# One core, cosformer attention followed by a swish MLP: chunk 1's output half plain and half in seven products, and another order and other stores for the last chunk

## The chip, the core and the metric

The kernel runs on one core of a Trainium2 chip. Its time is the device time of one launch in microseconds (us); lower is better. Engines are named as in the profile: PE (TensorE matmul), PEld (its weight load), DVE (VectorE), ACT (ScalarE), POOL (GpSimd) and SP (SyncE, which here only issues DMAs).

## What is computed

From q, k and v (8 batches, 8 heads, 576 positions, 64 features) a linear attention, whose result, 4608 tokens of 512, goes through an MLP with a swish whose slope is given by feature:

```python
r = np.maximum(x, 0.0); phi = np.concatenate([r * cos_w, r * sin_w], axis=-1)   # of q and of k
kv = np.einsum('bhsf,bhsd->bhfd', k_p, v); z = np.sum(k_p, axis=2)
attn = np.einsum('bhsf,bhfd->bhsd', q_p, kv) / (np.einsum('bhsf,bhf->bhs', q_p, z)[..., None] + 1e-06)
x = attn.transpose(0, 2, 1, 3).reshape(4608, 512)
h = x @ w_in                       # 512 -> 2048
g = h * (1.0 / (1.0 + np.exp(-beta * h)))
out = g @ w_out                    # 2048 -> 512
```

## The kernel before

**Chunks and batches.** The MLP works on 9 chunks (0 to 8) of 512 tokens; the attention on 8 batches of 576 tokens, which is nine blocks of 64. A batch is prepared while an earlier chunk is in the MLP. For a batch: q and k go through relu (L196, L199), v is scaled by cosine and sine (L202, 18 small pieces), relu(q) is transposed by a DMA on SP into `qt` (`q_turn_dma`, L251), `qs` is `qt` times a tangent (`tan_mul`, L221; by POOL in `q_tan`, L255, and for batch 2 by DVE at L827), `kv` is 144 small matmuls (`kv_mm`, L266), the attention's numerators are 144 more (`num_all`, L328, line L293 in the profile), and `x_part` (L779) divides them on DVE and sends them, transposed by a DMA on SP, into the chunk's `xt`.

**The MLP's two products.** A chunk makes 16 groups of `h` (128 features each), each followed by a silu on ACT into `g`, and then the output of four tiles of 128 tokens. A product is either plain (`h_group`, `h_plain`, `o_part`: matmuls of 512 columns) or by seven half-size products in place of eight (`h_fast`, `o_fast`: matmuls of 256 columns). For the latter DVE makes sums of the operands: S1 to S4 of `g` (`g_sum`, L390), T1 to T4 of `w_out` (`w_sums`, L803; T3 is written over a part of `wout`), and sums of `w_in` (`wh_sums`, L440) and of `xt`. `o_fast` (L536) returns named steps for one pair of token tiles (pair 0 is tiles 0 and 2, pair 1 tiles 1 and 3): "1" to "7" are products of eight matmuls on PE, c1, c5, cu and c4 are copies from PSUM by ACT, a2, a3 and a7 are additions on DVE that complete a part of the output and may release its store. "6", "7" and "4" add to the PSUM bank that "1" began, so "6" waits for c1, "7" for cu and "4" for a7.

**Which chunk does what.** Chunk 0 is plain. Chunk 1 makes `h` plainly (L811 to L827) and its output by two pairs of seven products (L840 to L865). Chunk 2 makes `h` plainly and its output by seven (L1014 to L1055). From chunk 3 on `chunk` (L917) walks a list written out by hand, `ORDER` for chunks 3 to 6 and `ORDER_END` for 7 and 8: a word such as `X6` is a step of an `h` pair, `p4` a plain group, `s12` a sum, `ox3` or `oy3` product "3" of output pair x (0) or y (1), `o3y` its a3 and `c4y` its c4. Each engine runs its instructions in the order of the program. Eight PSUM banks are shared by hand; the three numbers of a pair are the banks of "1/6/7/4", of "5/3" and of "2".

**Stores.** `store` (L506) writes a tile as two DMAs of 64 rows: from POOL up to chunk 6, then from SP; for the odd tiles of chunk 8 the second half is issued by ACT. In the last pair (`last`) c4 copies its 256 columns half by ACT and half by DVE, and a7's half of the tile is stored by itself.

**SPLITS** (L529) names, for chunks 2 to 5, how many groups of `h` and how many output products have their matmuls cut into two of half the columns: the same work in more instructions.

Of the kernel before, what the change touches and what calls it, by code (L numbers as in the profile page):

```python
# [13 lines left out]
ALU = mybir.AluOpType  # L14
PSUM = bass.MemoryType.PSUM

P = 128
NQ = 9
# [4 lines left out]
def kernel(  # L23
# [224 lines left out]
    def qs_of(b):  # L248
        return wx["q"] if b > 3 and b % 2 == 0 else qs_first
# [137 lines left out]
            gs[c, jt // 4] = gt_pool.tile([P, 4, TCH], BF16, name="g_t", tag="g_t")  # L387
        nc.scalar.activation(gs[c, jt // 4][:, jt % 4], ps[:, h_bank(c, jt)], AF.Silu, scale=beta[:, jt : jt + 1])  # L388

    def g_sum(c, i0, i1, kind):  # L390

        k_ = i0 // 2
        g_e, g_o = (gs[c, k_][:, 2 * (i0 - 2 * k_) + r : 2 * (i1 - 2 * k_) : 2] for r in range(2))
        hf = TCH // 2
        A11, A12, A21, A22 = g_e[:, :, 0:hf], g_o[:, :, 0:hf], g_e[:, :, hf:TCH], g_o[:, :, hf:TCH]
        s1, s2, s3, s4 = (t[:, i0:i1] for t in (S1, S2, S3, S4))
        o, l, r, op = {1: (s1, A21, A22, ALU.add), 2: (s2, s1, A11, ALU.subtract),
                       3: (s3, A11, A21, ALU.subtract), 4: (s4, A12, s2, ALU.subtract)}[kind]
        return nc.vector.tensor_tensor(o, l, r, op=op)  # L399

    def g_sums(c, i0, i1):
        for kind in (1, 3, 2, 4):
            got = g_sum(c, i0, i1, kind)
        return got

    def h_group(c, jt, cols=1):
# [33 lines left out]
    def wh_sums(jt):  # L440
        f0 = jt % 4
        A11, A12, A21, A22 = (win[jt // 4][:, 2 * jp : 2 * jp + 2, f * P : (f + 1) * P]
                              for f in (f0, f0 + 1) for jp in range(2))
        s1, s2, s3, s4 = (w_sum(jt, i) for i in range(4))
        nc.vector.tensor_tensor(s1, A21, A22, op=ALU.add)
        nc.vector.tensor_tensor(s3, A11, A21, op=ALU.subtract)
        nc.vector.tensor_tensor(s2, s1, A11, op=ALU.subtract)
        return nc.vector.tensor_tensor(s4, A12, s2, op=ALU.subtract)

    def x_sums(c):  # L450
        xt, n = xt_tile(c), NB // 2
# [51 lines left out]

    out_v = out.rearrange("(b p n) m -> b n p m", b=B, n=NQ)

    def store(c, tt, o_sb, m0=0, m1=DM):  # L506
        for hf in range(2):
            bb, n = divmod((c * TCH + tt * P) // HP + hf, NQ)
            eng = nc.gpsimd if c < 7 else (nc.sync, nc.scalar)[hf] if c == NTC - 1 and tt % 2 else nc.sync
            eng.dma_start(out=out_v[bb, n][:, m0:m1], in_=o_sb[hf * HP : (hf + 1) * HP, m0:m1])  # L510

    def o_mm(c, tt, jts, cols=1):
        o_ps = ps[:, (2, 3, 0, 1)[tt] if c == 0 else 2 + tt // 2]
# [12 lines left out]
    def o_part(c, tt, part, cols=1):  # L526
        o_mm(c, tt, range(4 * part, 4 * part + 4), cols)

    SPLITS = {2: (0, 11), 3: (5, 0), 4: (0, 8), 5: (3, 0)}  # L529
    made = {}  # L530

    def late(c):
# [3 lines left out]
    def o_fast(c, pr, banks):  # L536

        b_ps, e_ps, a_ps = (ps[:, k_, 0:HM] for k_ in banks)
        tok = slice(pr * P, (pr + 1) * P)
        last = c == NTC - 1 and pr == 1  # L540

        def prod(dst, left, right, start, stop, pieces=False):
            order = (0, 1, 2, 3, 4, 5, 7, 6) if c + 1 >= B else range(JT // 2)
            for i in order:
                w = HM // 2 if i and pieces else HM
                for m in range(0, HM, w):
                    nc.tensor.matmul(dst[:, m : m + w], lhsT=left(i), rhs=right[:, i, m : m + w],  # L547
                                     start=start and i == 0,
                                     stop=stop and i == order[-1], skip_group_check=True)

        def g_part(r, hf):
            def at(i):
                jt = 2 * i + r
                return gs[c, jt // 4][:, jt % 4, hf * (TCH // 2) + pr * P : hf * (TCH // 2) + (pr + 1) * P]
            return at

        def s_part(t):
            return lambda i: t[:, i, tok]

        o1 = osb_pool.tile([P, DM], FP32, name="o_sb", tag="o_sb")  # L560
        o2 = osb_pool.tile([P, DM], FP32, name="o_sb", tag="o_sb")
        p1 = part.tile([P, HM], FP32, name="p1", tag="p1")
        p5 = part.tile([P, HM], FP32, name="p5", tag="p5")
        u = part.tile([P, HM], FP32, name="u", tag="u")

        def c4():
            h = HM // 2 if last else HM
            nc.scalar.copy(o2[:, 0:h], b_ps[:, 0:h])
            if last:
                nc.vector.tensor_copy(o2[:, h:HM], b_ps[:, h:HM])  # L570
                store(c, pr + 2, o2, 0, HM)

        def stored(key, op):
            def do():
                op()
                waits[key[0]].discard(key[1:])
                if not waits[key[0]] and not (last and key[0] == "2"):
                    store(c, pr + (2 if key[0] == "2" else 0), o2 if key[0] == "2" else o1)
                if last and key == "2a7":
                    store(c, pr + 2, o2, HM, DM)  # L580
            return do

        waits = {"1": {"a2", "a3"}, "2": {"a7", "c4"}}
        add = dict(op=ALU.add)
        return {
            "1": lambda: prod(b_ps, g_part(0, 0), B11, True, False, late(c)),
            "5": lambda: prod(e_ps, s_part(S1), T1, True, False, late(c)),
            "6": lambda: prod(b_ps, s_part(S2), T2, False, False, late(c)),
            "2": lambda: prod(a_ps, g_part(1, 0), B21, True, True, late(c)),
            "7": lambda: prod(b_ps, s_part(S3), T3, False, False, late(c)),  # L590
            "3": lambda: prod(e_ps, s_part(S4), B22, False, True, late(c)),
            "4": lambda: prod(b_ps, g_part(1, 1), T4, False, True, late(c)),
            "c1": lambda: nc.scalar.copy(p1, b_ps),
            "c5": lambda: nc.scalar.copy(p5, e_ps),  # L594
            "cu": lambda: nc.scalar.copy(u, b_ps),
            "c4": stored("2c4", c4),
            "a2": stored("1a2", lambda: nc.vector.tensor_tensor(o1[:, 0:HM], a_ps, p1, **add)),
            "a3": stored("1a3", lambda: nc.vector.tensor_tensor(o1[:, HM:DM], e_ps, u, **add)),
            "a7": stored("2a7", lambda: nc.vector.tensor_tensor(o2[:, HM:DM], b_ps, p5, **add)),
        }  # L600
# [202 lines left out]
    def w_sums():  # L803
        z = ALU.subtract
        nc.vector.tensor_tensor(T1, B12, B11, op=z)
        nc.vector.tensor_tensor(T2, B22, T1, op=z)
        nc.vector.tensor_tensor(T4, B21, T2, op=z)
        nc.vector.tensor_tensor(T3, B22, B12, op=z)

    wx_tiles()  # L810
    for slot in range(16):  # L811
        h_group(1, slot)
        if slot == 0:
            num_rest()
            att_q(2)
            v_half(2, 0)
        if 3 <= slot < NQ:
            v_half(2, 1, slot, slot + 1, "act")
        if slot == 4:
            k_all(2)  # L820
            v_half(2, 1, 0, 3)
        elif slot == 6:
            w_sums()
        elif slot == 11:
            kv_all(2)
            for jp in range(2):
                tan_mul(nc.vector, qs_of(2)[:, jp], qts[0][:, jp], 0, NQ)  # L827
    q_relu(3, 0, "act")
    q_relu(3, 1, "act")
    q_turn_dma(3)  # L830

    def one_sums(kind):
        for i0 in range(0, JT // 2, 2):
            g_sum(1, i0, i0 + 2, kind)

    def ops(of, names):
        for n in names.split():
            of[n]()

    x, y = o_fast(1, 0, (2, 5, 4)), o_fast(1, 1, (3, 7, 6))  # L840
    ops(x, "1 c1")
    one_sums(1)
    ops(y, "1 c1")
    for t, bank in enumerate((4, 6, 0)):
        num_all(2, t, bank)
    one_sums(2)
    x_part(2, 0, 4)
    ops(x, "6 cu")
    ops(y, "6 cu")
    one_sums(3)  # L850
    ops(x, "2 5 c5")
    x_part(2, 1, 6)
    ops(x, "7")
    one_sums(4)
    ops(x, "a2 a7")
    ops(y, "7 2")
    got = wh_sums(0)
    x_part(2, 2, 0)
    load_raw(4, "q")
    q_tan(3, 0, got)  # L860
    q_tan(3, 1)
    ops(y, "a2 5 c5")
    ops(x, "3 a3 4 c4")
    ops(y, "a7 3 a3 4 c4")
    v_half(3, 0)  # L865

    def k_piece(b, j):
# [10 lines left out]
        "p7 s04 s13 V4 s22 SbV s23 sp7 s24 s31 s33 N0 k1 s32 ox1 c1o ox5 k3 c5o k2 ox6 s34 g0 g1 x0 k0 "  # L878
        "ox3 oy1 cuo c1y x2 o3x ox2 ox7 v8 oy5 x1 c5y o2x oy6 w8 q0 q1 cuy v2 v6 oy3 o7x v3 w1 oy7 w4 w3 "
        "w7 o7y ox4 v5 t3 w5 oy2 v4 c4x o3y v7 t1 w0 oy4 w6 t2 v1 c4y v0 o2y w2 t4")  # L880
    ORDER_END = (
        "E1 F1 E2 X1 c1E X5 c1X X2 E5 a2E c5X X6 E6 X3 c1F a2X Y1 cuX X7 c5E cuE c1Y E3 E7 Y6 a3X SaX cuY "
        "a7X a3E Y5 SaE a7E X4 F6 F5 Y7 c5Y E4 Y2 cuF c5F Y3 F7 F2 a7Y a3Y a7F SbX SbE Y4 F3 a2Y Z1 a2F "
# [33 lines left out]
    def chunk(c, b, x, y, parts):  # L917
# [22 lines left out]
            ({"q0", "q1"} | xs_all, q_next),  # L940
            ({f"{o}{n}" for o in "vw" for n in range(NQ)}, lambda: raw_next("v"))])
        last_sum = None
        for op in (ORDER if b < B else ORDER_END).split():
            n = int(op[-1]) if op[-1].isdigit() else None
            if op == "K":
                kv_mm(b, 0, 4)
# [59 lines left out]
    for c in range(2, NTC):  # L1006
        b = c + 1
        parts = (6, 0, 4) if c < FAST else (0, 6, 4)
        xb, yb = ((2, 3, 6), (1 if c == FAST - 1 else 7, 3, 6)) if c < FAST else ((3, 2, 0), (1, 2, 0)) if b < B else ((0, 3, 6), (1, 3, 6))
        x, y = o_fast(c, 0, xb), o_fast(c, 1, yb)  # L1010
        if c >= FAST:
            chunk(c, b, x, y, parts)
# [73 lines left out]
```

## Time and profile before

| | |
|---|---|
| median of 3 runs | 277.27 us (277.11 to 277.93) |
| the profiled execution | 277.93 us; span from first to last instruction 276.2 us |
| PE busy | 267.5 us (97%), 3745 matmuls |
| DVE, ACT, POOL busy | 221.2, 184.4, 67.8 us |
| granted TensorE clock | 1.000 |
| chunk 1: `h` groups, then output | 50.4 to 65.8 us, then 65.8 to 80.2 us |
| chunk 8: `h`, then output | 247.0 to 259.5 us, then 259.5 to 271.9 us |

The durations below come from the profiled execution, and times in us within it count from its first instruction. A busy PE is not yet PE at its peak, because the ends of matmuls are modelled; the distance from one matmul's start to the next is exact. The chain that ended last is followed back from the last instruction, at each step to what released it.

### The profile page before, as it was taken

What the parts mean: (1) busy time and instruction counts of PE and PEld (TensorE: products, weight loads), DVE (VectorE), ACT (ScalarE), POOL (GpSimd) and SP (SyncE); (2) the same over time, 40 slices, a digit from 0 to 9 for tenths busy, and PEclk for the clock granted to TensorE, in tenths of its full rate; (3) what the DMA queues carried; (4) which work ended last, traced back from release to release, by engine and by line L of the source; (5) the groups of instructions that cost most, each with busy time, mean ns of one, the idle gap of its engine ahead of it and who ended that gap; (6) DMA issues with size and microseconds to landing.
All of it is one profiled execution on the core that took longest, in us unless ns stands there. A gap on an engine that the chain in (4) does not pass through costs nothing.

```text
span 276.2 us, 9045 instructions
## 1 busy us (share of the span) xinstructions
PE 267.5 (97%) x3745; PEld 199.3 (72%) x3749; DVE 221.2 (80%) x579; ACT 184.4 (67%) x381; POOL 67.8 (25%) x87
## 2 busy tenths in 40 slices
PE   8799999999999999999999999999999999999993
PEld 8454455456875599869866898688768886888783
DVE  5989968599989899499958995899589589559832
ACT  5778757797238657697569856986595279439811
POOL 1444000600087073205520553044400140000000
PEclk9999999999999999999999999999999999999999
DMA  6999999999989999981899199905400740023006
GB/s 250 366 394 383 391 391 314 365 196 384 186 220 277 215 339 273 400 154 33 196 367 248 31 200 297 149 20 108 114 2 9 119 115 2 0 65 90 2 4 150
DMA packets 50585, 54.00 MB, mean 196 GB/s; under 512 B 31200, under 2 KB 31472, under 8 KB 50544
## 3 DMA queue, kind: packets, MB, share of 16 engines
q1 hardware_dynamic: 47584, 45.82, 60.2%
q0 software_dynamic: 2688, 7.34, 9.2%
q8 instruction: 29, 0.48, 0.8%
q10 hardware_dynamic: 272, 0.27, 0.4%
q14 instruction: 12, 0.10, 0.2%
HBM read 36.71 MB, written 9.44 MB: 167 GB/s over the span
## 4 chain that ended last, share of the span: by engine, by line
PE 80%; DMA 12%; DVE 3%; issue 1%; ACT 1%; SPq 1%; ACTq 0%; DVEq 0%
PE ps L547 31%; PE ps L468 16%; PE ps L422 13%; PE ps L380 11%; DMA raw_v<-in_v_dram 7%; DMA raw_q<-in_q_dram 5%; PE ps L293 3%; PE ps L517 3%; PE ps L272 2%; SPq L79 1%; DVE xs L315 1%; ACT vb L217 1%; PE ps L234 0%; PE ps L352 0%; DVE win L115 0%
## 5 line engine op out<-in xcount | busy, mean ns | idle before, releaser
L413 ACT ACTIVATE g_t<-ps,beta 128x512 bf16<-128x512 f32 x96 | 61.2, 699 | 2.9 <-DVE ps L498 2.8
L547 PEld LDWEIGHTS <-S 128*128 128x128 bf16 x589 | 51.3, 98 | 5.0
L510 POOL DMA_DIRECT2D out_dram<-o_sb x56 | 33.5, 604 | 66.6 <-ACT o_sb L523 24.6
L380 PE MATMUL ps<-xt,win 128*128 128x512 bf16 (+1 forms) x196 | 42.8, 375 | 0.1
L547 PEld LDWEIGHTS <-g_t 128*128 128x128 bf16 x440 | 38.2, 98 | 4.5 <-issue 0.4
L422 PE MATMUL ps<-xt,win 128*128 128x512 bf16 (+1 forms) x184 | 40.8, 351 | 0.0
L388 ACT ACTIVATE g_t<-ps,beta 128x512 bf16<-128x512 f32 x48 | 32.2, 690 | 7.9 <-PE ps L380 7.8
L380 PEld LDWEIGHTS <-win 128*128 128x128 bf16 x196 | 18.7, 98 | 21.1 <-issue 0.4
L547 PE MATMUL ps<-wout,g_t 128*128 128x256 bf16 (+1 forms) x284 | 31.8, 262 | 0.0
L547 PE MATMUL ps<-wout,S 128*128 128x256 bf16 (+1 forms) x305 | 31.5, 255 | 0.0
L547 PE MATMUL ps<-T,S 128*128 128x256 bf16 (+1 forms) x284 | 30.8, 262 | 0.0
L399 DVE TENSOR_TENSOR S<-g_t 128x512 bf16<-128x512 bf16 (+1 forms) x66 | 25.2, 412 | 4.1 <-ACT g_t L413 3.4
L217 ACT ACTIVATE vb<-raw_v,sin 128x256 bf16<-128x256 f32 (+1 forms) x61 | 27.4, 503 | 1.5 <-DMA raw_v<-in_v_dram 1.5
L222 POOL TENSOR_TENSOR qs<-qt,tanr 128x1152 bf16<-128x1152 bf16 x6 | 14.2, 2381 | 51.4 <-DVE den L304 29.8
L468 PEld LDWEIGHTS <-w_stage 128*128 128x128 bf16 x224 | 21.6, 98 | 6.9
L468 PE MATMUL ps<-w_stage 128*128 128x256 bf16 x168 | 26.5, 272 | 0.0
L422 PEld LDWEIGHTS <-win 128*128 128x128 bf16 x184 | 17.9, 98 | 10.1
L315 DVE TENSOR_TENSOR xs<-ps,rden 128x768 bf16<-128x768 f32 (+4 forms) x26 | 22.8, 884 | 0.8
L219 DVE TENSOR_SCALAR vb<-raw_v,cos 128x256 bf16<-128x256 f32 x63 | 20.6, 384 | 0.2
L594 ACT COPY p<-ps 128x256 f32<-128x256 f32 x16 | 6.0, 372 | 20.4 <-PE ps L547 20.4
L468 PEld LDWEIGHTS <-win 128*128 128x128 bf16 x168 | 16.4, 98 | 4.4 <-issue 0.4
L468 PE MATMUL ps<-xt,win 128*128 128x256 bf16 x112 | 19.1, 273 | 0.0
(106 smaller groups left out, 416.5 us busy)
## 6 DMA issues: line engine op xcount, KB each, us to landing
raw_v<-in_v_dram SPq DMA_DIRECT2D x7, 1152.0 KB, 10.3
raw_k<-in_k_dram SPq DMA_DIRECT2D x7, 1152.0 KB, 7.5
raw_q<-in_q_dram SPq DMA_DIRECT2D x7, 1152.0 KB, 7.8
out_dram<-o_sb POOLq DMA_DIRECT2D x56, 128.0 KB, 4.4
w_stage<-in_moe_w_in_dram SPq DMA_DIRECT2D x3, 1024.0 KB, 13.7
w_stage<-in_moe_w_out_dram SPq DMA_DIRECT2D x2, 1024.0 KB, 8.4
w_stage<-in_moe_w_out_dram SPq DMA_DIRECT2D x4, 512.0 KB, 11.9
out_dram<-o_sb SPq DMA_DIRECT2D x13, 128.0 KB, 2.4
```

The source lines that it names most:

```text
L217: nc.scalar.activation(o, a, AF.Copy, scale=t[:, n : n + 1])
L219: nc.vector.tensor_scalar(o, a, scalar1=t[:, n : n + 1], scalar2=None, op0=ALU.mult)
L222: return eng.tensor_tensor(dst.rearrange("q n (g p) -> q n g p", g=2), src.rearrange("q n (g p) -> q n g p", g=2), tanr[:, n0:n1].unsqueez ...
L315: nc.vector.tensor_tensor(o.rearrange("q j n s d -> q j (n s) d"), nv[:, :, a:z, :, 0:D].rearrange("q j n s d -> q j (n s) d"), rden[:, :, ...
L380: nc.tensor.matmul(ps[:, h_bank(c, jt), i * 64 : (i + w) * 64], lhsT=win[jt // 4][:, mi, (jt % 4) * P : (jt % 4 + 1) * P], rhs=xt[:, i : i ...
L388: nc.scalar.activation(gs[c, jt // 4][:, jt % 4], ps[:, h_bank(c, jt)], AF.Silu, scale=beta[:, jt : jt + 1])
L399: return nc.vector.tensor_tensor(o, l, r, op=op)
L413: nc.scalar.activation(gs[c, jt // 4][:, jt % 4], ps[:, bank], AF.Silu, scale=beta[:, jt : jt + 1])
L422: nc.tensor.matmul(ps[:, bank, o * 64 : z * 64], lhsT=win[jt // 4][:, mi, (jt % 4) * P : (jt % 4 + 1) * P], rhs=xt[:, o:z, jp, g * HP : (g ...
L468: nc.tensor.matmul(dst, lhsT=left[:, g], rhs=right[:, :, g * HP : (g + 1) * HP], start=start and g == 0, stop=stop and g == 1, skip_group_ ...
L510: eng.dma_start(out=out_v[bb, n][:, m0:m1], in_=o_sb[hf * HP : (hf + 1) * HP, m0:m1])
L547: nc.tensor.matmul(dst[:, m : m + w], lhsT=left(i), rhs=right[:, i, m : m + w], start=start and i == 0, stop=stop and i == order[-1], skip ...
```

## The change

Four things, in the order of the program.

1. **Chunk 1.** Pair 0 (tiles 0 and 2) is made plainly with `o_part`, whose matmuls after the first part are cut in two; pair 1 stays in seven products. The S sums are made for pair 1's tokens alone (`t0=P`: half the elements), three of four groups of them before `h` ends. T3 is made after the plain tiles. Batch 2's tangent product goes from DVE to POOL, behind T4; batch 3's relu(q) goes from ACT to DVE; batch 2's `kv` comes one group later; a piece of `v` goes from DVE to ACT.
2. **SPLITS** has other counts.
3. **Chunk 8** walks a list of its own, `ORDER_LAST`, and its pair y uses PSUM banks 1, 4, 7 in place of 1, 3, 6.
4. **The last stores.** c4 of the last pair is copied by ACT alone. a2's half of tile 1 is stored when it is done, both halves of the rows from SP; a3's half of it is stored by itself.

```diff
-    def g_sum(c, i0, i1, kind):
+    def g_sum(c, i0, i1, kind, t0=0):
...
-        A11, A12, A21, A22 = g_e[:, :, 0:hf], g_o[:, :, 0:hf], g_e[:, :, hf:TCH], g_o[:, :, hf:TCH]
-        s1, s2, s3, s4 = (t[:, i0:i1] for t in (S1, S2, S3, S4))
+        A11, A12, A21, A22 = g_e[:, :, t0:hf], g_o[:, :, t0:hf], g_e[:, :, hf + t0 : TCH], g_o[:, :, hf + t0 : TCH]
+        s1, s2, s3, s4 = (t[:, i0:i1, t0:] for t in (S1, S2, S3, S4))
...
-    def store(c, tt, o_sb, m0=0, m1=DM):
+    def store(c, tt, o_sb, m0=0, m1=DM, eng=None):
...
-            eng = nc.gpsimd if c < 7 else (nc.sync, nc.scalar)[hf] if c == NTC - 1 and tt % 2 else nc.sync
-            eng.dma_start(out=out_v[bb, n][:, m0:m1], in_=o_sb[hf * HP : (hf + 1) * HP, m0:m1])
+            own = nc.gpsimd if c < 7 else (nc.sync, nc.scalar)[hf] if c == NTC - 1 and tt % 2 else nc.sync
+            (eng or own).dma_start(out=out_v[bb, n][:, m0:m1], in_=o_sb[hf * HP : (hf + 1) * HP, m0:m1])
...
-    SPLITS = {2: (0, 11), 3: (5, 0), 4: (0, 8), 5: (3, 0)}
+    SPLITS = {2: (3, 10), 3: (3, 0), 4: (0, 7), 5: (5, 0)}
...
         def c4():
-            h = HM // 2 if last else HM
-            nc.scalar.copy(o2[:, 0:h], b_ps[:, 0:h])
+            nc.scalar.copy(o2[:, 0:HM], b_ps)
             if last:
-                nc.vector.tensor_copy(o2[:, h:HM], b_ps[:, h:HM])
                 store(c, pr + 2, o2, 0, HM)
...
-                if not waits[key[0]] and not (last and key[0] == "2"):
+                if not last and not waits[key[0]]:
                     store(c, pr + (2 if key[0] == "2" else 0), o2 if key[0] == "2" else o1)
-                if last and key == "2a7":
-                    store(c, pr + 2, o2, HM, DM)
+                elif last and key == "1a2":
+                    store(c, pr, o1, 0, HM, nc.sync)
+                elif last and key[1] == "a":
+                    store(c, pr + (2 if key[0] == "2" else 0), o2 if key[0] == "2" else o1, HM, DM)
...
-        if 3 <= slot < NQ:
+        if 2 <= slot < NQ:
             v_half(2, 1, slot, slot + 1, "act")
         if slot == 4:
             k_all(2)
-            v_half(2, 1, 0, 3)
+            v_half(2, 1, 0, 2)
         elif slot == 6:
-            w_sums()
-        elif slot == 11:
+            got = w_sums()
+        elif slot == 7:
+            q_tan(2, 0, got)
+            q_tan(2, 1)
+        elif slot == 12:
             kv_all(2)
-            for jp in range(2):
-                tan_mul(nc.vector, qs_of(2)[:, jp], qts[0][:, jp], 0, NQ)
-    q_relu(3, 0, "act")
-    q_relu(3, 1, "act")
-    q_turn_dma(3)
...
-    x, y = o_fast(1, 0, (2, 5, 4)), o_fast(1, 1, (3, 7, 6))
...
+        elif slot == 14:
+            att_q(3)
+            for k_ in range(3):
+                g_sums(1, 2 * k_, 2 * k_ + 2, P)
+    g_sums(1, 6, 8, P)
+    y = o_fast(1, 1, (2, 4, 3))
+    for k_ in range(8):
+        o_part(1, k_ // 4 * 2, k_ % 4, 2 if k_ > 0 else 1)
+        if k_ == 2:
+            for t, bank in enumerate((4, 6, 0)):
+                num_all(2, t, bank)
+            x_part(2, 0, 4)
+            x_part(2, 1, 6)
+    got = nc.vector.tensor_tensor(T3, B22, B12, op=ALU.subtract)
+    wh_sums(0)
     x_part(2, 2, 0)
     load_raw(4, "q")
     q_tan(3, 0, got)
     q_tan(3, 1)
...
+    for n in ("1", "c1", "5", "c5", "6", "cu", "2", "a2", "7", "a7", "3", "a3", "4", "c4"):
+        y[n]()
     v_half(3, 0)
...
+    ORDER_LAST = (
+        "E1 c1E E2 F1 X1 a2E c1X c1F X5 X2 E5 X6 c5X E6 cuX c5E cuE X3 a2X Y1 E3 X7 a3X c1Y a3E SaX a7X "
+        "E7 SaE F6 Y5 F5 a7E X4 Y2 c5F Y6 SbX F2 F3 a2Y c5Y a2F cuF E4 Z1 Y3 cuY SbE c1Z a3F Y7 F7 a3Y "
+        "SaF a7Y a7F V5 c5V SaY V1 Z6 Z5 Y4 V2 c1V SbY cuZ F4 Z2 V3 c5Z V6 Z3 p4 Z7 a2V cuV SbF sp4 a3V "
+        "p5 SaV a2Z sp5 a3Z SaZ p6 s13 s01 a7Z Z4 V7 p7 a7V V4 sp6 s11 s03 SbZ ox1 s21 s22 SbV sp7 oy1 "
+        "s12 s14 s31 ox2 c1o s32 s02 s34 oy2 s04 oy5 s33 c1y o2x s23 ox6 cuo o2y s24 ox5 ox7 c5y c5o o7x "
+        "ox3 oy6 cuy ox4 c4x oy7 o3x o7y oy3 oy4 o3y c4y")
...
-        for op in (ORDER if b < B else ORDER_END).split():
+        for op in (ORDER if b < B else ORDER_END if c + 1 < NTC else ORDER_LAST).split():
...
-        xb, yb = ((2, 3, 6), (1 if c == FAST - 1 else 7, 3, 6)) if c < FAST else ((3, 2, 0), (1, 2, 0)) if b < B else ((0, 3, 6), (1, 3, 6))
+        xb, yb = ((2, 3, 6), (1 if c == FAST - 1 else 7, 3, 6)) if c < FAST else ((3, 2, 0), (1, 2, 0)) if b < B else ((0, 3, 6), (1, 3, 6) if c + 1 < NTC else (1, 4, 7))
```

## The prediction, made before the changed kernel had run

> **What bounds the kernel now.** I read the page's busy shares and clock first, then the chain that ended last, then PE's start-to-start distances, and last the queues around each place that the diff touches.
>
> ```profile
> PE 267.5 (97%) x3745; PEld 199.3 (72%) x3749; DVE 221.2 (80%) x579; ACT 184.4 (67%) x381; POOL 67.8 (25%) x87
> PEclk9999999999999999999999999999999999999999
> q8 instruction: 29, 0.48, 0.8%
> ```
>
> PE is busy 97% of the span at full clock, so a change is worth what it does to PE's work, to PE's few holes, and to what follows the last matmul. After 64 us I find two holes of more than 0.2 us, both in reach of the change. The first, in the chain that ended last:
>
> ```profile
> 65.95 1.75 PE ps L547 x16
> 67.69 1.09 PE ps L293 x109
> 68.79 0.57 issue
> 69.36 0.44 PE ps L293 x27
> ```
>
> Sixteen matmuls of chunk 1's output, then batch 2's numerators, and in their midst PE stops (0.77 us from one start, 68.59, to the next, 69.36) and waits for nothing that the profile names. The third line of the first fence suggests the cause: 29 packets of instructions, 0.48 MB, and PE's program has 7,472 rows of weight load and matmul, so some 258 rows come in a packet. Numerators consume two rows in 8 ns, so some 1.0 us of them eat a packet. The trace has a packet starting at 66.85, 1.04 us long, and none until 73.55. I read the hole as PE waiting for instructions.
>
> The second hole is in chunk 2's output:
>
> ```profile
> 108.05 0.21 issue
> 108.25 0.42 DVE o_sb L599
> 108.68 0.04 issue
> 108.72 1.05 PE ps L547 x15
> ```
>
> Product "4" waits for a7, which stood behind other DVE work: 0.44 us. Elsewhere PE's matmuls follow each other at 109 ns (256 columns) or 216 ns (512). The end, by the timeline:
>
> ```profile
> 268.05 5.58 SPq L510 DMA_DIRECT2D out_dram<-o_sb  x7
> ...
> 270.82 1.04 PE L547 MATMUL ps<-T,g_t 128*128 128x256 bf16 x8
> 271.02 0.42 DVE L598 TENSOR_TENSOR o_sb<-ps,u 128x256 f32<-128x256 f32 x1 [0.58 <-PE ps L547]
> 272.12 0.27 ACT L568 COPY o_sb<-ps 128x128 f32<-128x128 f32 x1 [1.60 <-PE ps L547]
> 272.42 0.29 DVE L570 COPY o_sb<-ps 128x128 f32<-128x128 f32 x1 [0.98 <-ACT o_sb L568]
> 272.74 0.47 ACTq L510 DMA_DIRECT2D out_dram<-o_sb  x1
> ```
>
> The last copies are done at 272.71, and ACT issues its part of the last store at 272.74. But SP's part starts only at 273.08: SP issues without pause from 270.54 on (starts 270.54, 271.06, 271.74, 272.39, 273.08; 0.47 to 0.60 each). It lands at 275.24, ACT's at 275.07, and 0.97 later the span ends. So SP's queue is the end, by 0.17.
>
> **Chunk 1: PE's work, +0.86.** Before, 14 products of eight matmuls: 14 x 0.875 = 12.25. After, 7 products (6.13) and two plain tiles: five whole matmuls (5 x 0.216 = 1.08) and 54 cut ones (54 x 0.109 = 5.91), 13.11 in all. All of it is on the path.
>
> **Chunk 1: the first hole, -0.6.** The numerators no longer follow 1.75 us of output but 2.61 (4 x 0.216 + 16 x 0.109), so the same row is wanted 0.86 later; the run starts 8 rows later in the program, which at 4 ns is nothing. If the packet is asked for while `h` still runs, it is usable at 69.36 as before, wanted at 69.45, and the whole 0.77 goes. If it is asked for at a row inside the output, whose first matmuls are now twice as long, it comes up to 0.4 later and 0.3 of the hole stays. Nothing shows which; bounds -0.77 and 0 (the hole may move), I take -0.6, nearer to the first, because the packet started 0.9 us after the output did and other packets show a delay before they start. The Trainium skill ("Runtime: NRT & Kernel Launch", Instruction fetch mechanics) says that instructions come in blocks of 256 and that crossing a block is mostly hidden; the packet size agrees with 0.48 MB / 29, the hole does not. By "hidden" this term would be 0 and the sum 0.6 higher.
>
> **Chunk 1: does DVE keep up? 0.** Before, DVE was busy 13.04 of the 14.27 us. Now, in DVE's order and with its rows: T4 ends at 62.1. The `qt` of batch 2 lands at 62.43, so POOL's two tangent products (2 x 2.38) run to about 67.3. Batch 3's raw q lands at 66.02, and relu(q) on DVE reads it there, under POOL. What that does the trace shows once: nine pieces of `v` (L219) begin at 79.89 under a POOL product that ends at 81.80,
>
> ```profile
> L219 DVE TENSOR_SCALAR vb<-raw_v,cos x9: 343/344/2062, 79.9 to 83.7; 128x256 bf16<-128x256 f32 x9
> ```
>
> and the first takes 2.06 in place of 0.34: it waits until POOL is through. So the two relus (0.75, step 0.67) end near 68.5, as on ACT before (68.78). Then four groups of sums of 256 elements (chunk 2's take 0.93 from one group to the next): 72.3. Two divisions of 1.34: 74.9. T3 (1.22): 76.1; the plain tiles that still read that part of `wout` end at 74.3. `wh_sums(0)` (1.0): 77.0. The third division: 78.4. a2, then a7: 79.05. PE: 65.78 + 2.61 + 1.5 (numerators without hole) + 4.37 (five parts) = 74.26; "7", which wants T3, starts at 78.6 minus 0.88 = 77.7, 1.6 after T3; "4", which wants a7, starts at 79.5, 0.45 after a7. So no new wait, by a cover of 0.45; bounds 0 and +0.5, value 0. Behind "4" stand chunk 2's `h` groups, so any excess would count in full. ACT gains room (2.2 us of relu leave it, 0.5 of `v` come). SP: batch 3's transposition starts at 68.6 against 68.80, chunk 2's last input about 0.4 later than 78.53, for a chunk that starts at 80.2 or later. POOL's four earlier stores fall between.
>
> **The second hole, 0.** DVE's queue in chunk 2 follows PE and a `v` load that landed at 104.18, behind SP work that the change leaves where it is. Bounds -0.44 and +0.3; I take 0.
>
> **SPLITS, 0.** The cut matmuls cost 2.5 ns each (chunk 4's output, 168 matmuls, 12.47; chunk 3's, 112, 12.33), and the change has two matmuls fewer in all. What they move is where a packet ends: the numerators of chunks 3 to 6 begin within four rows of where they did. Chunk 3's run is already 0.12 longer than chunk 4's (1.50 against 1.38). Bounds -0.1 and +0.3, value 0.
>
> **Chunk 8's order, 0.** From 247.0 to 271.9 PE was busy 24.85 of 24.90. The products are the same in number, so a better order has nothing to win there. To lose: pair y's banks 4 and 7 must be free for "5" and "2". The last silu was done at 261.0, 1.5 after the output began; "2" of y starts 2.6 after it. "4" of y wants a7, which has the 0.875 of "3" for 0.42 of work and latency. Bounds 0 and +0.4, value 0.
>
> **The last stores, +0.32.** c4 in one piece takes 0.37 against 0.59 for the two halves, which ran one after the other; ACT's store goes out 0.22 sooner. But SP decides. Product x4 is now fourth from the end, not third, so SP begins pair x's second tile 0.875 sooner, at 269.67 for the same end of PE. Behind it then stand not five issues but seven, because tile 0's store comes after it (`o3x` stands after `oy7`). With the steps seen (0.52 within a tile, 0.64 to 0.69 between): 0.52 + 0.68 + 0.52 + 0.68 + 0.64 + 0.69 = 3.73, so the last issue starts at 273.40 in place of 273.08. Bounds -0.56 (SP empty: copy done 272.5, landing 2.16 later) and +0.6.
>
> **Sum.** 0.86 - 0.6 + 0.32 = +0.58. On the profiled execution (277.93) that is 278.5; it stands 0.66 above the median of the three runs, so I put the same difference on the median: 277.85. What can be told from no change is about 0.3%, 0.83 us: 276.44 to 278.10.
>
> **The rivals.**
>
> *The hole stays or moves* (instructions late whatever stands ahead): no -0.6, and another packet's hole of 0.1 to 0.3: 277.27 + 0.86 + 0.32 + 0.2 = 278.65. For it: the fetch is not under the program's control. Against: the later need is exactly of its size. Chance 0.2.
>
> *POOL catches DVE's sums* (the slower side). `wh_sums(0)` ends at 77.0, and POOL may start batch 3's products when `qt` lands, about 76.9. If DVE is 0.3 later than worked out, one sum waits as the L219 did, 2.4 for one POOL product or 4.7 for both; the third division, a7 and product "4" stand behind. Less the cover of 0.45: +2.0 and more, 279.9. It decides from 0.3 us of lateness on. Against: two POOL stores stand ahead of those products, and T3 is done 1.6 before its need. Here the trace shows only a tensor_scalar waiting, never a sum. The Trainium skill ("SBUF — State Buffer", Who interferes with whom) has a rule against this change: a DVE instruction with two SBUF inputs also contends with a GpSimd instruction that reads SBUF. By it the sums can be caught as L219 was; if only L219's kind can be, the sum stays at 277.85. Chance 0.12.
>
> *Everything gives*: both holes go and the single copy shortens the end: 0.86 - 0.77 - 0.44 - 0.2 = -0.55, 276.7. For it: stores spread over more time. Against: SP's count. Chance 0.1.
>
> *The order does nothing*, as I hold for PE, is in the forecast.
>
> **Numbers.** Forecast case 0.55, mostly 277.3 to 278.3; the rest to a stall of a few tenths in chunk 8. Range 276.8 to 279.0: it leaves out the port case and the edge of the good one. Faster by over 0.3%: 0.06, half of the good case's. Slower: the first rival, the port case and the forecast's upper end (a cover gone), 0.2 + 0.12 + 0.07 = 0.39. Within: 0.55.
>
> **What would show it.** Chunk 1's output 13.1 us without numerators; no "issue" near 69; a7 of pair 1 before product "4" is due; `wh_sums` of 0.29 each; the SP issues of the end unbroken from c4x to the last, 0.3 later after PE's end than now. Wrong if the numerators still break, if a DVE sum takes over 1 us, or if SP's last issue follows at once on c4.

## The result and the profile after

The changed kernel took 280.46 us (median of 4 executions, 279.81 to 281.29) beside 277.6 for the kernel before (4 executions): a ratio of 1.0104, 95% interval 1.0068 to 1.0139. Run once more it took 280.13 beside 277.96 (1.0077, 1.0056 to 1.0097). It is slower by 2 to 3 us where 277.85 was forecast, with no change as the likeliest, and it lies outside the range given.

The page of the profiled execution (280.43 us, span 278.6), engines and clock:

```profile
PE 269.9 (97%) x3741; PEld 200.9 (72%) x3747; DVE 217.4 (78%) x574; ACT 182.5 (66%) x378; POOL 70.6 (25%) x89
PEclk9999999999999999999999999999999999999998
```

PE still decides: the same share, the full clock but for the last slice (0.996 on the mean), four matmuls fewer by the records and 2.4 us more. So the loss must stand in PE's line, stage by stage, and behind its last matmul. First the place where before had stopped, in the chain that ended last (columns: start, length, what):

```profile
66.06 2.56 PE ps L517 x19
68.62 1.47 PE ps L293 x141
70.09 0.98 PE ps L517 x8
```

The numerators (L293) run through, without the 0.57 of "issue" near 69. The same view 27 us later, in batch 3's numerators:

```profile
95.76 1.07 PE ps L293 x105
96.83 0.74 issue
97.57 0.48 PE ps L293 x32
```

There the stop is again, in another chunk. In chunk 5 the chain stayed on PE before:

```profile
180.12 0.22 PE ps L468 x2
180.33 1.38 PE ps L293 x133
```

After, it leaves PE:

```profile
180.25 0.41 issue
180.66 0.45 DVE ps L498
...
181.13 1.27 ACT g_t L413 x2
...
182.45 0.59 PE ps L293 x37
```

An addition of DVE (L498, a3 of the last `h` pair) starts 0.41 late with nothing to wait for that the profile shows; the last silu (L413) and PE stand behind it. In chunk 8 the chain leaves PE once:

```profile
251.98 1.93 PE ps L468 x17
...
253.92 0.45 DVE ps L498
...
254.41 2.56 PE ps L468 x22
```

PE waits for a3 of pair F: 0.35 from start to start in place of 0.11, so 0.24 is lost. Last, the timeline of the end, SP's queue and then ACT (start, length):

```profile
271.34 4.55 SPq L510 DMA_DIRECT2D out_dram<-o_sb  x7
```
```profile
273.79 0.37 ACT L567 COPY o_sb<-ps 128x256 f32<-128x256 f32 x1 [2.47 <-PE ps L547]
274.19 0.47 ACTq L510 DMA_DIRECT2D out_dram<-o_sb  x1
```

Seven issues of SP in one row, as forecast; the copy is done at 274.16 and SP's part of that store starts at 275.33. The trace has PE's last matmul end at 273.52, the last landing at 277.35 and the span's end at 278.63. The tail, from PE's end to the span's end, is 5.11, against 4.30 before.

Since single executions differ, this table has one row for each of eleven profiles. A chunk's length is the distance from its first `h` matmul to the next chunk's (for chunk 8, to PE's end); chunks 3, 4 and 6 differ by 0.15 at most; chunk 0 (33.17 to 34.01) and the time ahead of it (16.47 to 17.26) differ by execution in both families; they are left out. The labels are those of the experiments below.

| profile | chunk 1 | chunk 2 | chunk 5 | chunk 7 | chunk 8 | tail |
|---|---|---|---|---|---|---|
| before | 29.99 | 29.39 | 28.01 | 24.91 | 25.07 | 4.30 |
| before again (h4) | 29.34 | 30.25 | 28.09 | 24.92 | 25.07 | 4.27 |
| before with the new chunk 8 (e2) | 29.33 | 29.48 | 28.37 | 24.91 | 25.31 | 5.11 |
| after | 30.22 | 30.19 | 28.39 | 25.03 | 25.31 | 5.11 |
| after with the old chunk 8 (e1) | 30.22 | 29.26 | 28.37 | 25.05 | 25.07 | 4.26 |
| after, POOL later (f2) | 30.20 | 29.26 | 28.39 | 25.03 | 25.31 | 5.12 |
| after, o3x first (f3) | 30.23 | 30.73 | 29.14 | 25.04 | 25.31 | 4.23 |
| after, three repairs (g1) | 30.22 | 29.26 | 28.02 | 24.91 | 25.31 | 4.23 |
| the same, V1 first (h2) | 30.18 | 30.56 | 28.02 | 24.91 | 25.23 | 4.23 |
| f2, numerators earlier (h3) | 30.68 | 29.26 | 28.40 | 25.03 | 25.31 | 5.11 |
| after, sums later (g3) | 33.77 | 30.86 | 28.37 | 25.03 | 25.31 | 5.11 |

Read down the columns: chunks 7 and 8 and the tail follow the program to a few hundredths. Chunk 2 does not: 29.26 to 30.86 within one family. Not all of that is one thing: in after and f3 PE stops inside the numerators, in h4 and h2 it waits in the output, for a copy of ACT (0.4) and for a division of DVE (0.9). (e2's 28.37 in chunk 5 is a stop of PE in the numerators, 0.36 from start to start; its addition L498 is not late.) One execution of f1, 285.89, ran at a granted clock of 0.949 and is left out of the table and of the count of executions below; the ratios leave out it and those more than 1.5% above their kernel's fastest, the medians leave out none.

### The profile page after: what moved, and what is told of

Same layout as the page of the kernel before. It is cut to its first block, busy times and chain, and to the rows that moved or that the text cites. A ratio compares the mean times of both kernels' runs of the same rounds, so it can differ in the third digit from the quotient of the medians.

```text
span 278.6 us, 9033 instructions
## 1 busy us (share of the span) xinstructions
PE 269.9 (97%) x3741; PEld 200.9 (72%) x3747; DVE 217.4 (78%) x574; ACT 182.5 (66%) x378; POOL 70.6 (25%) x89
## 4 chain that ended last, share of the span: by engine, by line
PE 86%; DMA 5%; DVE 4%; issue 1%; ACT 1%; ACTq 0%; DVEq 0%
PE ps L547 31%; PE ps L468 15%; PE ps L422 12%; PE ps L380 12%; DMA raw_q<-in_q_dram 5%; PE ps L517 5%; PE ps L293 3%; PE ps L272 3%; PE ps L605 1%; PE ps L234 1%; PE ps L609 1%; DVE qb L194 1%; DVE xs L315 1%; ACT g_t L413 0%; PE ps L619 0%
## 5 line engine op out<-in xcount | busy, mean ns | idle before, releaser
L413 ACT ACTIVATE g_t<-ps,beta 128x512 bf16<-128x512 f32 x96 | 61.1, 702 | 3.6 <-DVE ps L498 3.4
L547 PEld LDWEIGHTS <-S 128*128 128x128 bf16 x550 | 48.2, 98 | 4.7
L510 POOL DMA_DIRECT2D out_dram<-o_sb x56 | 31.3, 565 | 73.9 <-ACT o_sb L523 31.7
L547 PEld LDWEIGHTS <-g_t 128*128 128x128 bf16 x409 | 35.7, 98 | 3.9 <-issue 0.3
L380 PEld LDWEIGHTS <-win 128*128 128x128 bf16 x205 | 19.6, 98 | 20.2 <-issue 0.2
L547 PE MATMUL ps<-wout,g_t 128*128 128x256 bf16 (+1 forms) x261 | 29.7, 264 | 0.0
L547 PE MATMUL ps<-wout,S 128*128 128x256 bf16 (+1 forms) x282 | 29.4, 257 | 0.0
L547 PE MATMUL ps<-T,S 128*128 128x256 bf16 (+1 forms) x268 | 28.7, 262 | 0.0
L222 POOL TENSOR_TENSOR qs<-qt,tanr 128x1152 bf16<-128x1152 bf16 x8 | 19.0, 2395 | 37.4 <-DVE den L304 30.4
L399 DVE TENSOR_TENSOR S<-g_t 128x512 bf16<-128x512 bf16 (+1 forms) x66 | 24.3, 395 | 4.0 <-ACT g_t L413 2.7
L422 PEld LDWEIGHTS <-win 128*128 128x128 bf16 x184 | 17.9, 98 | 10.2
L517 PE MATMUL ps<-wout,g_t 128*128 128x512 bf16 (+1 forms) x117 | 21.6, 330 | 0.4 <-issue 0.2
L468 PEld LDWEIGHTS <-win 128*128 128x128 bf16 x168 | 16.4, 98 | 4.7 <-issue 0.2
```

The costliest lines, as they stand in the source:

```text
L380: nc.tensor.matmul(ps[:, h_bank(c, jt), i * 64 : (i + w) * 64], lhsT=win[jt // 4][:, mi, (jt % 4) * P : (jt % 4 + 1) * P], rhs=xt[:, i : i ...
L413: nc.scalar.activation(gs[c, jt // 4][:, jt % 4], ps[:, bank], AF.Silu, scale=beta[:, jt : jt + 1])
L422: nc.tensor.matmul(ps[:, bank, o * 64 : z * 64], lhsT=win[jt // 4][:, mi, (jt % 4) * P : (jt % 4 + 1) * P], rhs=xt[:, o:z, jp, g * HP : (g ...
L468: nc.tensor.matmul(dst, lhsT=left[:, g], rhs=right[:, :, g * HP : (g + 1) * HP], start=start and g == 0, stop=stop and g == 1, skip_group_ ...
L510: (eng or own).dma_start(out=out_v[bb, n][:, m0:m1], in_=o_sb[hf * HP : (hf + 1) * HP, m0:m1])
L517: nc.tensor.matmul(o_ps[:, m0 : m0 + w], lhsT=gs[c, jt // 4][:, jt % 4, tt * P : (tt + 1) * P], rhs=wout[:, jt, m0 : m0 + w], start=(jt == ...
```

## The experiments

Sixteen runs in four groups (e, f, g, h), each group beside runs of the kernel before of its own: medians 277.85, 277.96, 278.39 and 277.97. In brackets stand the ratio to these and its 95% interval.

**First: which half.** e1 is the changed kernel with before's chunk 8 and stores, e2 the kernel before with the new ones.

```diff
 # e1, against after (in part); e2 is the reverse, against before
-        for op in (ORDER if b < B else ORDER_END if c + 1 < NTC else ORDER_LAST).split():
+        for op in (ORDER if b < B else ORDER_END).split():
...
-            nc.scalar.copy(o2[:, 0:HM], b_ps)
+            h = HM // 2 if last else HM
+            nc.scalar.copy(o2[:, 0:h], b_ps[:, 0:h])
```

> Chunk 1 and SPLITS as after; chunk 8's list, its banks, c4 and the last stores as before. If the parts add up as the two traces say (up to the end of chunk 7 the changed kernel is 1.4 us later, of it 0.9 from a PE hole in chunk 2's numerators and 0.4 from one in chunk 5's, and 1.0 comes from chunk 8 and the stores): 1.0 to 1.5 us over the kernel before, with the hole at about 96.6 us again. Rival, that the larger part is in chunk 8 and the stores: under 0.5 over the kernel before.

> The kernel before with after's chunk 8 list, banks, c4 and last stores alone. By the traces: chunk 8's h part 0.2 longer (a PE wait for DVE near 254), from PE's end to the span's end 0.4 to 0.7 longer, so 0.6 to 1.0 us over the kernel before, and no hole in chunk 2's numerators. By the prediction's sum: 0.32 over. Rival, that the new list and the single copy gain: not slower than before.

e1 279.12 (1.0034, 1.0019 to 1.0050); e2 278.53 (1.0027, 0.9999 to 1.0055). By the medians the halves cost 1.27 and 0.68, together 1.95; e2's interval just reaches no change, but its profile holds the cost. In the table e2 pays chunk 8's 0.24 and the tail's 0.81, e1 0.89 in chunk 1, 0.36 in chunk 5 and 0.13 in chunk 7, each against the shortest of before's rows.

**SPLITS.** e3 is after with before's counts, e4 before with (4, 11) for chunk 2, which shifts PE's rows as after does; f4 is after with the rows of chunk 2 shifted back.

```diff
 # e3
-    SPLITS = {2: (3, 10), 3: (3, 0), 4: (0, 7), 5: (5, 0)}
+    SPLITS = {2: (0, 11), 3: (5, 0), 4: (0, 8), 5: (3, 0)}
 # e4 (before)
-    SPLITS = {2: (0, 11), 3: (5, 0), 4: (0, 8), 5: (3, 0)}
+    SPLITS = {2: (4, 11), 3: (5, 0), 4: (0, 8), 5: (3, 0)}
 # f4
-    SPLITS = {2: (3, 10), 3: (3, 0), 4: (0, 7), 5: (5, 0)}
+    SPLITS = {2: (0, 12), 3: (3, 0), 4: (0, 7), 5: (5, 0)}
```

> After with before's SPLITS: chunk 2's numerators begin at row 2475 of PE's program (before 2469, after 2493). Theory that the place in the program decides: the instruction block that begins at row 2712 is wanted 18 rows deeper in the run and asked for as in the kernel before, the hole of 0.93 at 96.6 shrinks below 0.3, about 0.8 us faster than after (279.7 against 280.5). Rival, that DMA traffic which chunk 1's part moved holds up the packet: the hole stays at 0.8 to 0.9 and the time that of after.

> The kernel before with the matmuls of chunk 2's first four h groups cut as well (12 matmuls, 24 rows more; 0.03 us of work): its numerators begin at row 2493, as in after, with before's traffic. Place theory: a hole of about 0.9 at 96.6, 0.9 us over the kernel before (or less by what the shift does to later runs, which all move by 24 rows: each may gain or lose a hole of its own). Traffic theory: the packet starts at 91.8 as in the kernel before, no hole there, and the same time within 0.2 unless a later run meets a block's edge.

> The changed kernel with chunk 2's three cut groups of h made whole and two more output products cut (SPLITS of chunk 2 (0, 12) in place of (3, 10)): chunk 2's numerators begin 18 rows earlier in PE's program, later chunks' 10 rows later; PE's work changes by under 0.05. Theory 'where an instruction block ends inside the numerators decides': the hole at 96.6 (0.91 in the changed kernel's profile) is 0.2 or less, and the median is 0.5 to 0.9 under the changed kernel's. Rival 'the hole comes and goes by execution whatever the row': the same median within 0.3.

e3 282.51 (1.0120, 1.0050 to 1.0190), e4 278.79 (1.0026, 1.0003 to 1.0048), f4 280.71 (1.0094, 1.0064 to 1.0125). e3 cannot be read for SPLITS: in its profile POOL catches two sums of DVE in chunk 1 (2.48 and 2.35 for 0.28), and PE stands 4.6. f4's profile has no stop in chunk 2's numerators, but f2's, with the rows of after, has none either, and f4's time did not fall. That the row at which a block ends decides chunk 2 was my theory, and it fell: of ten profiles with after's rows two have the stop there (after and f3). Whether the row helps is open, because e4's profile has a stop of 0.38 there and the five with before's rows (before, e2, g4, h1, h4) have none; e4 is slower than before, but its rows alone do not tell why.

**Do the parts add, and does POOL catch sums?** f1 is the changed kernel unedited; f2 starts POOL's product of batch 3 behind wh_sums.

```diff
 # f2
-        nc.vector.tensor_tensor(s4, A12, s2, op=ALU.subtract)
+        return nc.vector.tensor_tensor(s4, A12, s2, op=ALU.subtract)
...
-    got = nc.vector.tensor_tensor(T3, B22, B12, op=ALU.subtract)
-    wh_sums(0)
+    nc.vector.tensor_tensor(T3, B22, B12, op=ALU.subtract)
+    got = wh_sums(0)
```

> The changed kernel once more, unedited, beside the kernel before on one chip. Theory 'the parts add': chunk 1 with SPLITS alone was 1.27 above before in its median (279.12 against 277.85), chunk 8 with its stores alone 0.68 (278.53), so both together 1.95 above before; the 280.46 of the first runs was then a few executions with the 0.9 hole in chunk 2's numerators that the profile showed. Rival 'the hole belongs to the changed program': 2.7 to 2.9 above before, no execution under 2.0. If POOL sometimes catches a DVE sum in chunk 1, one execution in ten or so is 3 to 6 us above the rest.

> The changed kernel with POOL's product of batch 3 waiting for the last of the sums of w_in (wh_sums) in place of T3. Theory 'POOL sometimes catches DVE's sums': the same median as the changed kernel within 0.4, no execution more than 2 us above it, and in the profile all four sums of w_in take 0.28 to 0.31. Rival 'POOL's start is harmless, the outliers come from elsewhere': outliers stay at the same rate. Rival 'POOL is then late for batch 3': the median rises by 0.5 or more.

f1 280.13, 2.17 above before, against 1.95 for the sum of the halves: they add as far as the noise lets one see (f1's interval is 1.6 to 2.7). f2 279.75 (1.0065, 1.0039 to 1.0092), none above 281.4. g3 then forces the catch:

```diff
 # g3
-    wh_sums(0)
     x_part(2, 2, 0)
+    wh_sums(0)
```

> The changed kernel with the four sums of w_in (wh_sums) behind batch 2's third division in place of ahead of it, so that they start about 1.3 later, at 77.3, when POOL's product of batch 3 (from about 76.7 on) is running. Theory 'a DVE sum with two operands in SBUF waits until POOL's product is through': in every execution one or two of the sums take 1.5 to 2.5 in place of 0.28, a7 and product 4 of chunk 1 stand behind them, and the time is 3.5 to 4.5 above the changed kernel's, 283.6 to 284.6. Rival 'only a tensor_scalar waits for POOL, a sum does not': the same time within 0.5. Rival 'POOL's product then merely starts later': within 0.5 as well, with POOL's start after 78.5 in the profile.

g3 284.52 (1.0206, 1.0169 to 1.0242), all six from 283.3 to 285.0, as the first theory had it. Its timeline, DVE and then POOL:

```profile
77.29 2.31 DVE L445 TENSOR_TENSOR w_stage<-win 128x256 bf16<-128x256 bf16 x1
79.52 2.46 DVE L446 TENSOR_TENSOR w_stage<-win 128x256 bf16<-128x256 bf16 x1
81.90 0.28 DVE L447 TENSOR_TENSOR w_stage<-w_stage,win 128x256 bf16<-128x256 bf16 x1
```
```profile
77.06 4.76 POOL L222 TENSOR_TENSOR qs<-qt,tanr 128x1152 bf16<-128x1152 bf16 x2 [0.40 <-DMA qt<-qb]
```

In g3 and e3 a sum that began between POOL's start and its end was held until the product running was done. In the changed kernel's own profile it is a matter of 0.06:

```profile
76.58 0.29 DVE L448 TENSOR_TENSOR w_stage<-win,w_stage 128x256 bf16<-128x256 bf16 x1
```
```profile
76.64 4.82 POOL L222 TENSOR_TENSOR qs<-qt,tanr 128x1152 bf16<-128x1152 bf16 x2
```

`qt` landed at 76.47 there, and POOL's queue passed the product's last wait at 76.64, after the last sum had started. In g2's profile (its edit is below) `qt` landed at 75.72, the wait was passed at 76.14, and a sum that started at 76.29 was held for both products, although POOL, busy with two stores, began the first at 76.62 by the profile, whose spans on POOL are rough. The chain there:

```profile
76.17 0.20 DVE w_stage L446
76.37 5.14 DVE w_stage L447
```

Of 64 executions of kernels with after's chunk 1 and POOL's early start (g3 aside), nine took over 283 us; of 42 with POOL behind wh_sums, none. The two caught ones with a profile show the catch; for the others it is an inference.

**The end.** f3 moves o3x ahead of c4x in the new list; g4 tries the like on before, with the single copy.

```diff
 # f3
-        "ox3 oy6 cuy ox4 c4x oy7 o3x o7y oy3 oy4 o3y c4y")
+        "ox3 oy6 cuy ox4 o3x c4x oy7 o7y oy3 oy4 o3y c4y")
 # g4 (before)
-        "o7x oy5 c5y ox4 c4x t2 o7y oy3 t4 t3 o2y o3y oy4 c4y")
+        "o7x oy5 c5y ox4 o7y c4x t2 oy3 t4 t3 o2y o3y oy4 c4y")
...
-            nc.scalar.copy(o2[:, 0:h], b_ps[:, 0:h])
+            nc.scalar.copy(o2[:, 0:HM], b_ps)
             if last:
-                nc.vector.tensor_copy(o2[:, h:HM], b_ps[:, h:HM])
```

> The changed kernel with one step moved in chunk 8's list: o3x, which releases tile 0's store, ahead of c4x. Theory 'SP's queue in order is the end': a3 of pair x was done at 269.62 but its store stood behind c4x's until 271.34; moved ahead, two of seven issues go out 1.7 earlier, the last store is issued right after c4's copy (0.64 after PE's end in place of 1.8), and the tail from PE's end to the end of the span goes from 5.11 to 3.9 to 4.1: 1.0 to 1.2 faster than the changed kernel. Rival 'the copy and the landing are the end': 0.3 or less. Rival 'before's tail (4.30) is the floor': 0.8.

> The kernel before with its end alone changed: c4 of the last pair copied by ACT alone, and o7y's step (its store) ahead of c4x's. Theory 'the end is SP's queue in order': a7 of pair y was done at 270.10 but its store stood behind c4x's until 271.74; ahead of them SP has issued all by the time c4 is copied, the last store goes out 0.65 after PE's end in place of 1.22, the tail of the span is 3.9 to 4.2 in place of 4.30, and the time is 0.2 to 0.4 under before. Rival 'the tail cannot go under 4.25 whoever is first': no change within 0.1.

f3 279.82 (1.0051, 1.0020 to 1.0082), tail 4.23. ACT's timeline:

```profile
275.18 0.37 ACT L567 COPY o_sb<-ps 128x256 f32<-128x256 f32 x1 [2.50 <-PE ps L547]
275.58 0.50 ACTq L510 DMA_DIRECT2D out_dram<-o_sb  x1
```

The last copy ends at 275.55 and both ACT's and SP's part of that store start at 275.58, which for SP is 0.69 after PE's end in place of 1.81: in the changed kernel tile 0's data were ready at 269.62, but its store stood in SP's queue behind one that was ready only at 271.31. The issue is 1.1 earlier, the tail 0.88 shorter, because the last landing is ACT's, 2.22 after its issue, and 1.33 more pass to the end. That is nearer to the rival's 0.8 than to my 1.0 to 1.2. By the medians only 0.3 is seen (0.7 by the ratios): f3's profile holds more stops in chunks 2 and 5 than after's. g4 278.41 (0.9996, 0.9971 to 1.0021), tail 4.25: nothing. I had miscounted: behind c4x with the last there still stood four issues, started from 272.32 to 274.17, for a copy done at 273.64.

**Chunk 5's addition, and the repairs together.** DVE's program has four instructions fewer ahead of chunk 5's L498 in every kernel with the new chunk 1. g2 puts four idle writes back; g1 has them with f2's and f3's edits.

```diff
 # g2
             q_tan(2, 0, got)
             q_tan(2, 1)
+            pad = const.tile([P, 4], FP32, name="pad")
+            for i in range(4):
+                nc.vector.memset(pad[:, i : i + 1], 0.0)
```

> The changed kernel with the four writes on DVE alone. In chunk 5 the addition L498 that the last silu waits for started 0.60 to 0.67 after the one before it in all profiles of kernels whose DVE program has 4 instructions fewer ahead of it, and 0.25 in all three with as many as before. Theory 'DVE waits there for a block of its instructions, and the four missing instructions put the block's end at this addition': its gap is 0.25 again, the 0.4 at 180.25 in the chain is gone, PE's hole at about 182 is 0 to 0.35, and the median is 0.3 to 0.4 under the changed kernel's. Rival 'the gap comes from the changed data flow of chunk 1': gap still 0.6, same median.

> The changed kernel with three repairs: POOL's product of batch 3 behind wh_sums, o3x ahead of c4x, and four writes of one column into a tile that nothing reads, put on DVE in chunk 1 where it is idle (so that DVE's program has its instructions of chunk 5 at the places that they have before). Theory 'the loss is the sum of places': from the changed kernel's 2.17 above before (280.13 against 277.96) go 0.87 of the tail and 0.38 of chunk 5: 0.9 above before, no execution more than 2.5 above it. Rival 'the instruction holes move on and take the gain': 1.4 or more above before.

The addition in the timelines, of after and then of g1 (in brackets the idle time before it and the releaser that the profile names):

```profile
179.62 0.42 DVE L497 TENSOR_TENSOR ps<-ps,p 128x256 f32<-128x256 f32 x1
180.66 0.43 DVE L498 TENSOR_TENSOR ps<-ps,u 128x256 f32<-128x256 f32 x1 [0.62 <-PE ps L468]
```
```profile
179.19 0.42 DVE L497 TENSOR_TENSOR ps<-ps,p 128x256 f32<-128x256 f32 x1
179.86 0.43 DVE L498 TENSOR_TENSOR ps<-ps,u 128x256 f32<-128x256 f32 x1 [0.25 <-PE ps L468]
```

The releaser named is PE in both, but its product was no later in after. The idle time is 0.60 to 0.67 in all nine profiles without the four instructions and 0.25 in all nine with them (before and its five variants, g1, g2, h2). I read this as an instruction block of DVE that ends just ahead of the addition. The packets fit: in the nine profiles with the late addition a packet of the second instruction queue (q14) starts 0.47 to 0.95 after the addition does; in the nine others none starts within 4 us after it. Chunk 5 loses 0.37 by it, and chunk 7's 0.12 goes with the same four writes. As a time g2 shows nothing: 281.29 (1.0089, 1.0056 to 1.0121), several of its 11 executions far up and its profile a caught one. g1 278.99 beside 278.39 (1.0021, 0.9993 to 1.0049): of 2.17 some 0.6 is left, less than the 0.9 expected, and that is no longer clear of the noise.

**What is left.** h2 is g1 with V1 ahead of V5 in chunk 8; h3 is f2 with the numerators one part earlier; h1 is before with x2 ahead of the numerators; h4 is before again.

```diff
 # h2
-SaF a7Y a7F V5 c5V SaY V1 Z6
+SaF a7Y a7F V1 V5 c5V SaY Z6
 # h3
-        if k_ == 2:
+        if k_ == 1:
 # h1
-    x, y = o_fast(1, 0, (2, 5, 4)), o_fast(1, 1, (3, 7, 6))
+    x, y = o_fast(1, 0, (2, 5, 1)), o_fast(1, 1, (3, 7, 6))
...
     ops(y, "1 c1")
+    ops(x, "2")
...
-    ops(x, "2 5 c5")
+    ops(x, "5 c5")
```

> The kernel with the three repairs and in chunk 8's list V1 ahead of V5, c5V and SaY. In all profiles with the new list PE stood 0.24 at 254 for a3 of pair F, which still read the bank that V5 writes. Theory 'the list's order costs this 0.24': V1's 0.44 covers the wait, no hole near 254, 0.2 to 0.3 under the kernel with three repairs (278.99 beside a before of 278.39), so 0.3 to 0.4 above before. Rival 'the wait moves to the next step': a hole of 0.1 to 0.24 behind V5 or SaY, same time.

> The changed kernel with POOL's product behind wh_sums, and batch 2's numerators after two parts of chunk 1's plain tiles in place of three, which is 1.73 behind the start of the output, as before had them (1.75). Theory 'the block is late by the clock': the stop inside these numerators is back, 0.5 to 0.8 long, and the time is 280.2 to 280.6 against the 279.75 of the same kernel with three parts. Rival 'the hole belonged to before's rows or execution': no stop, 279.75 within 0.3.

> The kernel before with one product of chunk 1 (x2, into bank 1 in place of 4) moved ahead of batch 2's numerators, so that these begin 0.875 later behind the start of chunk 1's output, with no work added. Theory 'the hole at 68.6 is a block of instructions that is late by the clock': the numerators run without the 0.77 stop, chunk 1's output takes 13.6 to 13.7 in place of 14.44, and the time is 0.5 to 0.8 under before, if DVE, which has about 0.7 of slack in this stage, keeps up. Rival 'the block is asked for by the rows run': the hole stays as it is, the time is the same within 0.2. Rival 'DVE is the next bound': the hole goes and 0.3 to 0.7 of it comes back as a wait for a7 or a sum before chunk 2.

> The kernel before once more, for a second profile of it. Theory 'chunk 1's hole and DVE's block ends are fixed by the program, the holes in chunk 2 and PE's in chunk 5 come and go': a stop of 0.6 to 0.9 near 68.6 again, L498 in chunk 5 with a gap of 0.25, a tail of 4.25 to 4.35, and a hole of a different size in chunk 2's output. Rival 'all of them come and go': no stop near 68.6 or a gap of 0.6 in chunk 5.

In h1 the numerators of bank 0, which reach into bank 1, are written over x2's product, so a part of chunk 1's output is lost; the instructions and their order are those described. h2 278.71 (1.0025, 1.0008 to 1.0043), chunk 8 25.23 in place of 25.31: the wait shrank by 0.08 and the time shows no gain. h1 278.38 (1.0018, 0.9996 to 1.0039). h4 278.06 (0.9998, 0.9980 to 1.0016). h3 280.10 (1.0092, 1.0068 to 1.0115), with the stop back in its chain:

```profile
67.71 1.12 PE ps L293 x112
68.83 0.40 issue
69.23 0.41 PE ps L293 x26
```

That spoke for my theory of the late block. But h4, the very kernel before, has no stop there; its chain:

```profile
66.36 1.75 PE ps L547 x16
68.11 1.36 PE ps L293 x138
69.47 0.04 issue
69.51 2.56 PE ps L547 x22
```

Of five profiles with before's chunk 1 (before, h4, e2, e4, g4) only the first has it. Its packet of instructions started 1.1 after chunk 1's output did, in the other four 0 to 0.45 after. So there was nothing for h1 to win, and it won nothing. A late packet is not before's alone: it started 1.0 after chunk 1's output in f2 and 1.15 in after, 1.05 in h3. In f2 and after the numerators begin 2.49 behind the output and run through; in before (1.84) and h3 (1.83) they stop. No kernel here beats before.

## Why the prediction was wrong

- **"Chunk 1: PE's work, +0.86": right.** Chunk 1 takes 30.20 to 30.23 in six profiles and 29.33 to 29.34 in the three of before's family in which nothing stops: 0.88.
- **"The first hole, -0.6": the step that failed first.** Against the profile shown, chunk 1 did lose only 0.23 net. But the hole belonged to that execution, not to the kernel: in four of five profiles with before's chunk 1 there is nothing to save, and a change cannot save what most executions do not pay. That later numerators cover a late packet was right (after and f2 against before and h3); that before's packet is late as a rule was not. There was a hint: that execution was 0.66 above the median, about the hole's size, and I carried the 0.66 over as a constant difference. Like stops come and go in later numerators: after's 0.74 at 96.83 had its packet start 0.8 before the numerators, f2, without a stop, 3.7 before; before's family has them in chunk 2 (e4), chunk 3 (h1) and chunk 5 (e2, g4). In each of these stops, before's first among them, PE went on 1.3 to 1.5 after the end of the packet begun last, which fits the reading that it waits for instructions. What makes a packet late is open; the row (f4) was not shown to decide it.
- **"Does DVE keep up? 0": right in most executions, and the rival "POOL catches DVE's sums" is real.** DVE's times came out within 0.4 (relus until 68.41, sums until 72.14, T3 until 75.94, a7 until 79.45). The point from which it decides was only half seen: the sums race with `qt`'s landing, which moved from 75.7 to 78.2 between profiles; in after's own it was won by 0.06. The rule of the Trainium skill that the prediction set against this ("SBUF — State Buffer", Who interferes with whom) agrees with g3: sums of two SBUF operands took 2.31 and 2.46 in place of 0.28. It costs some executions 3 to 6 and the median little (f2 against f1: 0.4).
- **"SPLITS, 0", where I looked at packets of PE alone.** The counts themselves cost nothing that shows (chunks 3 and 4 within 0.15). But chunk 1 leaves DVE's program four instructions shorter, and with these missing the addition on which chunk 5's last silu waits is late: 0.37, and 0.12 in chunk 7. No term stood for it. The Trainium skill ("Runtime: NRT & Kernel Launch", Instruction fetch mechanics) has the crossing of a block mostly hidden, as the prediction quotes it; this one was not, in nine profiles of nine, if the late addition is one.
- **"The second hole, 0": right.** a7's wait went from 0.44 to 0.31.
- **"Chunk 8's order, 0": low, within its bounds.** 0.24 in every profile with the list; another place for V1 takes 0.08 of it away (h2).
- **"The last stores, +0.32": right in mechanism, too small.** It was 0.81, beyond the bound of 0.6. The last issue came 0.59 later relative to PE's end, not 0.32: the six steps between the seven issues took 3.99, not 3.73. It landed 0.15 faster. And from the last landing to the end of the span passed 1.28 in place of 0.92 (the prediction's 0.97 was read 0.05 too long), since seven of SP's closing waits (0.06 each) ended after it, where before one did.

The sum, from the profiles: 0.88 + 0.37 + 0.12 + 0.24 + 0.81 = 2.42, give or take what chunk 2 does in an execution. Measured, by the medians: 2.17 and 2.86. The forecast had 0.58. None of the rivals is what happened: "the hole stays or moves" (278.65) has the right doubt about the hole and lacks the rest.

## What to carry to other kernels

A stop that one profile shows belongs to that execution until a second profile has it too, the more so if the execution is above the median by the stop's size; count it as saved only then. In a queue that issues in order, put a store where its data are ready: a step moved past one that was not ready yet cost 0.9 at this kernel's end. Four instructions more or fewer on an engine can move a wait in a much later stage: here on DVE, from chunk 1 to chunk 5; for PE's rows no run here shows a cost that is theirs alone.

## What the runs showed of the hardware that I had not expected

- An addition on the path began 0.35 to 0.42 later in all nine profiles in which DVE's program was four instructions shorter ahead of it, and four idle writes 117 us earlier took this away. That a block of instructions ends there is inferred, from the packets and the count.
- A DVE sum that meets POOL's products can be held for both at once (g2: 5.14, for 4.7 of POOL), or slip in between them (g3: 2.31, then 2.46). In g2 the sum began 0.15 after POOL's queue had passed the product's waits and, by the profile, 0.33 before the product.
- From the last landing to the end passed 0.90 to 0.92 where one of SP's closing waits ended after it (before, e1), and 1.28 to 1.35 where seven or eight did (after, e2, f3, g1).
